# Whole-row loads of the streamed key and value weights, and the order of the loads and stores around the tail multiplications

## The chip, the cores and the metric

The kernel runs on one core of one Trainium2 chip. The metric is the device time of one execution in microseconds (us), from the first to the last instruction. Three runs of the kernel before took 3842.35, 3847.23 and 3854.59 us, so the median is 3847.23 us. The profiled execution took 3842.35 us and its trace spans 3840.6 us.

The engines are named as in the profile: PE is the matrix engine (PEld its weight loads), DVE the vector engine, ACT the scalar engine, POOL GpSimd, and SP the engine that here only issues DMA transfers.

## The reference

Four layers run one after the other on 2048 tokens of width 640: A, B, A, B, each with a layer norm ahead of it and a residual added behind it. All tensors are bf16. The A layer is recurrent over 64 segments of 32 tokens, and each segment takes 8 memory tokens from the one before:

```python
def _A_ref(x, mem0, Wq, Wk, Wv, Wo, seg_len):          # 32 heads of 192
    mem = mem0
    for s in range(n_seg):                             # 64 segments
        h = concatenate([mem, xs], axis=1)             # 8 + 32 tokens
        q, k, v = (einsum('btd,dhe->bhte', h, W) for W in (Wq, Wk, Wv))
        p = softmax(where(mask, q @ k.T * scale, -1e9))
        o = einsum('bhte,hed->btd', p @ v, Wo)
        mem = o[:, :M, :]                              # the chain from segment to segment
        outs.append(o[:, M:, :])
```

The B layer is a linear attention over all 2048 tokens (qkv of width 1920, a small feature map per head, one `kv` sum, then the output product). It can only start on rows whose A output is there.

## The kernel before

**The chain of A.** 6144 output features are worked on in four rounds of 8 heads (`r`, each 1536 columns wide). Most of the weights lie in SBUF for good. For rounds 0 and 3, three of the five contraction pieces of each of Q, K and V share a place (a slot) and so are loaded anew in every segment, as is the output weight of the round that comes last. The last 8 tokens of every segment (the tail) don't take part in the chain's output product. Their attention outputs are stored to DRAM (`otb`) and multiplied with the output weight after the chain.

```python
PW = 1536
def load_slot(m, r, b, whole=False):
    if holds.get((m, b)) != r:
        holds[m, b] = r
        w = PW if whole or m == "Q" else PW // 2
        for h in range(0, PW, w):                       # K and V in the chain: two halves
            nc.sync.dma_start(out=slot[m, b][:, h:h + w], in_=wview[m][:, b, PW * r + h:PW * r + h + w])

def project(hT, ps, m, n, s, steps):                    # round n of segment s
    for i in steps:
        b = (i + KC - ns) % KC if n == 0 else i         # n == 0: the slots first
        w = piece(m, r, b)
        for g in range(4):
            ...                                         # rhs of K and Q: columns of both halves
            nc.tensor.matmul(o[32 * g:32 * g + 32, 0:384], lhsT=hT[:, b, :], rhs=rhs, ...)
        if n == 0 and b >= KC - ns:
            load_slot(m, order[NR - 1], b)              # for the last round of the same segment
```

A segment issues its transfers on SP in this order: Q slots, K slots, V slots (all freed in round 0, read again in round 3), then the six pieces of the last output weight (freed by the first `wo_round`, read by the last):

```python
wo_round(W, order[n - 1], OT, n == 1, False)
if n == 1:
    load_wo(order[L])                                   # six pieces of 320 KB
```

**The start of B.** The stored tails come back in four blocks of 16 segments (1.5 MB each). `fetch` loads a block, `spread` reorders it by four copies, two on ACT and two on DVE, and `multiply` does 48 x 2 matmuls and stores 128 rows to `at_dram` (`attn`). The rows of B are then read back from `attn`, normed (`norm_rows`) and transposed (`turn_rows`).

```python
with tc.issue_after(self.last_load.ins):
    load_rows(0)
fetch, spread, multiply = post
ot = [fetch(tb) for tb in range(2)]
ow = [spread(tb, ot[tb]) for tb in range(2)]
ot += [fetch(tb) for tb in range(2, 4)]
for j in (1, 2, 0):
    nc.sync.dma_start(out=wqkv[:, :, D * j:D * j + D], in_=...)
multiply(0, ow[0], kv_ps[0], side_bank("ps_post"))
ow.append(spread(2, ot[2]))
rows = [norm_rows(b) for b in range(4)]
multiply(1, ow[1], ...)
ow.append(spread(3, ot[3]))
multiply(2, ow[2], ...)
first_xnT = new_xnT()
for b in range(4):
    turn_rows(b, rows[b], first_xnT)
multiply(3, ow[3], ...)
```

Blocks 0 and 2 share one buffer, blocks 1 and 3 the other. The order in which instructions of B stand on an engine is set by the scheduler of the language, so the order of the text is a priority and not a promise. The instructions of one engine then run in that order.

Of the kernel before, what the change touches and what calls it, by code (L numbers as in the profile page):

```python
# [112 lines left out]
class Kernel:  # L113
# [131 lines left out]
    def layer_B(self, x_dram, at_dram, xout_dram, xnext_dram, li, bp, post):  # L245


        nc, tc, KC, D = self.nc, self.tc, self.KC, self.Dm
# [41 lines left out]
        with tc.tile_pool(name=f"B{li}_kv", bufs=1, space=bass.MemoryType.PSUM, reuse_waits="tile") as kvp, \  # L290
# [5 lines left out]
            def side_bank(name):  # L296
                return ptp.tile([P, 512], F32, name=name, tag="side")

            nc.gpsimd.memset(wbd[:], 0.0)
            for i in range(HC):  # L300
                n = len(range(i, H, HC))
                nc.gpsimd.dma_start(out=wbd[DH * i:DH * i + DH, 0:n, DH * i:DH * i + DH],
                                    in_=self.B_w_phi[i:H:HC].rearrange("h d f -> d h f"))
# [45 lines left out]
            def load_rows(g):  # L349
                for b in range(4 * g, 4 * g + 4):  # L350
                    nc.sync.dma_start(out=x2[:, b, :], in_=x_dram[P * b:P * b + P, :])

            def norm_rows(b):
                xt = x2[:, b, :]
                al = als.next()
                nc.sync.dma_start(out=al[:], in_=at_dram[P * b:P * b + P, :])
                nc.gpsimd.tensor_tensor(out=xt, in0=xt, in1=al[:], op=ALU.add)  # L357
                xn = xns.next()
                self.ln_rows(bp, xt, xn, scale=nc.scalar)
                return xn  # L360
# [90 lines left out]

            with tc.issue_after(self.last_load.ins):
                load_rows(0)
            fetch, spread, multiply = post
            ot = [fetch(tb) for tb in range(2)]
            ow = [spread(tb, ot[tb]) for tb in range(2)]
            ot += [fetch(tb) for tb in range(2, 4)]
            for j in (1, 2, 0):
                nc.sync.dma_start(out=wqkv[:, :, D * j:D * j + D],
                                  in_=self.B_wqkv.rearrange("(k p) n -> p k n", p=P)[:, :, D * j:D * j + D])  # L460
            multiply(0, ow[0], kv_ps[0], side_bank("ps_post"))
            ow.append(spread(2, ot[2]))
            rows = [norm_rows(b) for b in range(4)]
            multiply(1, ow[1], kv_ps[1], side_bank("ps_post"))
            ow.append(spread(3, ot[3]))
            multiply(2, ow[2], kv_ps[0], side_bank("ps_post"))
            first_xnT = new_xnT()
            for b in range(4):
# [11 lines left out]
            for sg in range(2):  # L480
                for c in range(NC_):
                    mc, nh = sizes[c], sizes[c] // DH
                    o = kv_out(sg, c).rearrange("p (h f) -> p h f", f=DH + 1)
# [88 lines left out]
    def layer_A(self, xn_dram, at_dram, li, x_raw=None):  # L572
        nc, tc = self.nc, self.tc
        KC, NSEG = self.KC, self.NSEG
        dram = self.dram
        NR = 4
        PW = 1536
        self.kqb_d = dram.tile([NSEG, P, NR, 192], BF16, name=f"kqb{li}")
        self.vb_d = dram.tile([NSEG, NR, 2, 8, 896], BF16, name=f"vb{li}")
        self.otb_d = dram.tile([NSEG, P, 384], BF16, name=f"otb{li}")  # L580
        wview = self.wview
        wov = self.A_Wo.rearrange("h d m -> (h d) m").rearrange("(c p) m -> p c m", p=P)
        low = self.view(0, LATE)
        at = LATE
        res, slot = {}, {}
        for r in (3, 2):
            for m in "KQV":
                for b in range(KC - (SLOTS[m] if r == 3 else 0)):
                    res[m, r, b] = low[:, len(res) * PW:len(res) * PW + PW]
        assert len(res) * PW * 2 == LATE  # L590
        for m, r, b in [(m, 0, b) for m in "KQV" for b in range(KC - SLOTS[m])] + \
                [(m, None, b) for m in "KQV" for b in range(KC - SLOTS[m], KC)] + [(m, 1, b) for m in "KQV" for b in range(KC)]:
            v = self.view(at, 2 * PW)
            at += 2 * PW
            if r is None:
                slot[m, b] = v
            else:
                res[m, r, b] = v
        holds = {}
        wo_mid = self.view(at, 24 * 1280)  # L600
        wo_end = self.view(at + 24 * 1280, 12 * 1280)
        assert at + 36 * 1280 == ARENA
        unread = set(res)

        def load_slot(m, r, b, whole=False):
            if holds.get((m, b)) != r:
                holds[m, b] = r
                w = PW if whole or m == "Q" else PW // 2
                for h in range(0, PW, w):
                    nc.sync.dma_start(out=slot[m, b][:, h:h + w], in_=wview[m][:, b, PW * r + h:PW * r + h + w])  # L610

        def load_matrix(m, r):
            for b in range(KC):
                if (m, r, b) in unread:
                    unread.remove((m, r, b))
                    nc.sync.dma_start(out=res[m, r, b], in_=wview[m][:, b, PW * r:PW * r + PW])
                elif (m, r, b) not in res:
                    load_slot(m, r, b, True)

        early = {(0, 5), (2, 4), (2, 5), (1, 0), (1, 1), (1, 2), (1, 3)}  # L620

        def load_wo(r, into=None, part=range(6)):
            t = into if into is not None else wo_end[:, :] if r in (0, 3) else wo_mid[:, 7680 * (r - 1):7680 * r]
            for k in part:
                tk = t[:, 1280 * k:1280 * k + 1280]
                if r in (0, 3):
                    self.last_load = nc.sync.dma_start(out=tk, in_=self.wo_rows[r // 3, :, 1280 * k:1280 * k + 1280])
                else:
                    nc.sync.dma_start(out=tk.rearrange("p (c m) -> p c m", m=640),
                                      in_=wov[:, 12 * r + 2 * k:12 * r + 2 * k + 2, :])  # L630

        def piece(m, r, b):
            assert (m, r, b) in res or holds[m, b] == r
            return res[m, r, b] if (m, r, b) in res else slot[m, b]

        def lay_out_wo():
            if li == 0:
                self.wo_rows = dram.tile([2, P, 7680], BF16, name="wo_rows")
                for i, r in enumerate((0, 3)):
                    nc.scalar.dma_start(out=self.wo_rows[i].rearrange("p (c m) -> p c m", m=640),  # L640
                                        in_=wov[:, 12 * r:12 * r + 12, :])

        def early_wo():
            for r in (0, 2, 1):
                load_wo(r, part=[k for k in range(6) if (r, k) in early])

        def late_wo(r):
            load_wo(r, part=[k for k in range(6) if (r, k) not in early])

        self.A_pre(xn_dram, li, load_matrix, piece, wo_mid, wo_end, lay_out_wo, early_wo, x_raw)  # L650
        self.A_chain(xn_dram, at_dram, li, load_slot, piece, load_wo, late_wo, wo_mid, wo_end, low)
        self.post_args = at_dram, wo_mid, wo_end, low

# [445 lines left out]
    def post_steps(self, ops):  # L1099

        nc = self.nc
        at_dram, wo_mid, wo_end, low = self.post_args
        wo = [wo_end[:, :], wo_mid[:, 0:7680], wo_mid[:, 7680:15360], low[:, 0:7680]]

        def fetch(tb):
            o = 7680 + 12288 * (tb % 2)
            ot = low[:, o:o + 6144].rearrange("p (s f) -> p s f", f=384)
            nc.sync.dma_start(out=ot, in_=self.otb_d[16 * tb:16 * tb + 16].rearrange("s p f -> p s f"))
            return ot

        def spread(tb, ot):
            o = 7680 + 12288 * (tb % 2)
            ow = low[:, o + 6144:o + 12288].rearrange("p (c q) -> p c q", q=P)
            for k in range(4):
                self.ev.copy(out=ow[:, 12 * k:12 * k + 12, :].rearrange("p c (s t) -> p c s t", t=8),
                             in_=ot[:, :, 96 * k:96 * k + 96].rearrange("p s (c t) -> p c s t", t=8))
            return ow

        def multiply(tb, ow, p0, p1):
            for c in range(48):  # L1120
                lhsT = ow[:, c, :]
                w0 = 640 * (6 * (c % 2) + c % 12 // 2)
                w = wo[c // 12][:, w0:w0 + 640]
                nc.tensor.matmul(p0[:, :], lhsT=lhsT, rhs=w[:, 0:512], start=(c == 0), stop=(c == 47))  # L1124
                nc.tensor.matmul(p1[:, 0:128], lhsT=lhsT, rhs=w[:, 512:640], start=(c == 0), stop=(c == 47))
            ob = ops.tile([P, 640], BF16, name="obB", tag="obB", bufs=2)
            nc.vector.tensor_copy(out=ob[:, 0:512], in_=p0[:, :])
            nc.scalar.activation(out=ob[:, 512:640], in_=p1[:, 0:128], func=ACT.Copy)
            av = at_dram.rearrange("(s t) d -> s t d", t=32)
            nc.gpsimd.dma_start(out=av[16 * tb:16 * tb + 16, 24:32, :], in_=ob[:, :])  # L1130

        return fetch, spread, multiply


# [33 lines left out]
```

## Time and profile before

| | us | share of the span |
|---|---|---|
| span of the trace | 3840.6 | |
| PE busy | 3561.2 | 93% |
| DVE busy | 2327.9 | 61% |
| ACT busy | 2075.0 | 54% |
| POOL busy | 1668.6 | 43% |
| queue 1 (transfers issued on SP), share of 16 DMA engines | | 60.7% |
| first chain of A, from about 212 us to 1629 us | 1417 | 37% |
| second chain of A, from about 2112 us to 3521 us | 1409 | 37% |

The page cuts the span into 40 equal slices and writes the busy share of each as a digit. Groups of instructions follow with their line of the kernel, the names of output and inputs, the shapes, the count, the busy time, the mean of one in ns, and the idle time just ahead of them with what ended it. A wait is written "who line <- what it waited for: us in total, times, longest us". "issue" stands where the profile shows nothing that was waited for. Among the chain's loads the page counts 768 issues of K and 768 of V with 192 KB each; those are the halves.

### The profile page before, as it was taken

To read this page: it belongs to the slowest core of one execution; us is meant where nothing else is said; L and a number is where in the kernel's file an instruction comes from. 1 tells how busy PE (TensorE), PEld (TensorE's weight loads), DVE (VectorE), ACT (ScalarE), POOL (GpSimd) and SP (SyncE) were. 2 spreads that over 40 slices of the span, in tenths; PEclk is the share of its full clock that TensorE was granted. 3 is DMA by queue.
4 is the path that set the end of the run, shared out by engine and by line. 5 is a ranking of instruction groups with operands and counts; after the bars stand their busy time and mean duration, and the time that the engine had idled before them with its cause. 6 is when DMAs were issued, how large, how long until landed. Compare 5 with 4: busy or idle time off the path is not lost. (4 is left out here: it accounts for less than half of the span.)

```text
span 3840.6 us, 167757 instructions
## 1 busy us (share of the span) xinstructions
PE 3561.2 (93%) x70296; PEld 2244.8 (58%) x70312; DVE 2327.9 (61%) x6038; ACT 2075.0 (54%) x5285; POOL 1668.6 (43%) x4375
## 2 busy tenths in 40 slices
PE   7889999999999999989899899999999999999798
PEld 5656566666666565545367556666666666665453
DVE  3546666666666666545643566666666666664464
ACT  2245666556655565536432556566665656664453
POOL 2435454455544454430242444555455454553300
PEclk9999999999999999989899999999999999999898
DMA  9787888888888887840377878888888888889100
GB/s 323 243 266 271 283 281 282 277 268 292 275 281 277 270 288 264 298 134 1 120 246 201 296 268 285 274 285 282 280 283 268 284 272 283 282 278 298 48 1 28
DMA packets 587137, 935.19 MB, mean 243 GB/s; under 512 B 147322, under 2 KB 401802, under 8 KB 586378
## 3 DMA queue, kind: packets, MB, share of 16 engines
q1 hardware_dynamic: 448042, 804.45, 60.7%
q0 software_dynamic: 68672, 90.26, 8.0%
q10 hardware_dynamic: 69664, 29.76, 2.9%
q8 instruction: 551, 9.03, 1.0%
q14 instruction: 208, 1.70, 0.1%
HBM read 855.97 MB, written 72.09 MB: 242 GB/s over the span
## 5 line engine op out<-in xcount | busy, mean ns | idle before, releaser
L884 PE MATMUL ps_qk<-arena,hT 128*32 128x384 bf16 x20480 | 1004.1, 328 | 24.6 <-DMA arena<-in_A_Wk_dram 7.3
L884 PEld LDWEIGHTS <-hT 128*32 128x32 bf16 x30720 | 742.6, 97 | 472.8 <-DVE hT L1094 59.1
L894 ACT ACTIVATE raw<-ps_qk 128x384 bf16<-128x384 f32 x1024 | 503.0, 491 | 442.2 <-PE ps_s L987 248.9
L960 PE MATMUL ps_w<-arena,OT 128*32 128x160 bf16 x24576 | 552.8, 235 | 65.2 <-issue 36.3
L867 POOL DMA_DIRECT2D Vp<-vb x512 | 258.7, 505 | 675.4 <-PE ps_o L934 463.2
L960 PEld LDWEIGHTS <-OT 128*32 128x32 bf16 x24576 | 437.8, 97 | 184.0 <-issue 90.7
L884 PE MATMUL ps_v<-arena,hT 128*32 128x384 bf16 x10240 | 538.4, 330 | 0.6 <-issue 0.5
L899 DVE STREAM_TRANSPOSE KT<-raw 128x384 bf16<-128x384 bf16 x512 | 296.1, 578 | 199.3 <-ACT raw L894 195.3
L902 DVE STREAM_TRANSPOSE QT<-raw 128x256 bf16<-128x256 bf16 x512 | 227.9, 445 | 269.2 <-ACT raw L894 240.6
L855 POOL DMA_DIRECT2D kqb<-kqb x512 | 290.0, 566 | 168.6 <-POOL KT L863 146.6
L915 DVE CAST Vp<-ps_v 64x384 bf16<-64x384 f32 x512 | 286.0, 559 | 99.0 <-ACT Vp L913 84.4
L953 POOL DMA_DIRECT2D otb<-otb x512 | 282.5, 552 | 133.7 <-DVE otb L949 105.0
L913 ACT ACTIVATE Vp<-ps_v 64x384 bf16<-64x384 f32 x512 | 246.3, 481 | 150.9 <-PE ps_v L884 117.5
L940 DVE CAST OT<-ps_o 128x192 bf16<-128x192 f32 x512 | 183.1, 358 | 215.2 <-PE ps_o L934 197.3
L934 PEld LDWEIGHTS <-Vp 80*128 80x128 bf16 x4096 | 182.6, 99 | 189.0 <-issue 128.5
L994 DVE TENSOR_TENSOR E<-E,ps_s 80x320 bf16<-80x320 bf16 x512 | 247.5, 483 | 73.9 <-ACT ps_s L993 69.3
L973 ACT ACTIVATE E<-ps_s 80x320 bf16<-80x320 f32 x512 | 221.8, 433 | 114.6 <-PE ps_s L926 102.0
L934 PE MATMUL ps_o<-E,Vp 80*128 80x80 bf16 x4096 | 235.3, 202 | 26.6 <-issue 4.7
L926 PE MATMUL ps_s<-QT,KT 128*80 128x80 bf16 (+1 forms) x3072 | 234.7, 214 | 22.3 <-DVE KT L899 13.0
L860 POOL COPY QT<-kqb 128x64 bf16<-128x64 bf16 x512 | 125.6, 245 | 283.2 <-PE ps_s L926 279.6
L967 PE MATMUL ps_idle<-arena,ident 128*128 128x384 bf16 x1024 | 235.0, 332 | 5.0 <-issue 5.0
L939 ACT ACTIVATE OT<-ps_o 128x192 bf16<-128x192 f32 x512 | 167.8, 328 | 131.4 <-PE ps_o L934 131.3
(148 smaller groups left out, 5348.5 us busy)
## 6 DMA issues: line engine op xcount, KB each, us to landing
arena<-wo_rows SPq DMA_DIRECT2D x792, 320.0 KB, 5.9
arena<-in_A_Wq_dram SPq DMA_DIRECT2D x430, 384.0 KB, 4.5
arena<-in_A_Wk_dram SPq DMA_DIRECT2D x768, 192.0 KB, 5.4
arena<-in_A_Wv_dram SPq DMA_DIRECT2D x768, 192.0 KB, 5.2
kqb<-arena ACTq DMA_DIRECT2D x16, 1536.0 KB, 11.3
kqb<-kqb POOLq DMA_DIRECT2D x512, 48.0 KB, 5.0
arena<-in_A_Wk_dram SPq DMA_DIRECT2D x46, 384.0 KB, 6.7
arena<-in_A_Wv_dram SPq DMA_DIRECT2D x46, 384.0 KB, 8.2
```

Of the source, the lines that this page charges most:

```text
L855: nc.gpsimd.dma_start(out=kqb[:], in_=self.kqb_d[s, :, r, :])
L867: nc.gpsimd.dma_start(out=Vs[n % 2][64:80, :], in_=self.vb_d[s, r].rearrange("g t f -> (g t) f"))
L884: nc.tensor.matmul(o[32 * g:32 * g + 32, 0:384], lhsT=hT[:, b, :], rhs=rhs, start=(i == 0), stop=(i == KC - 1), tile_position=(0, 32 * g), ...
L894: nc.scalar.activation(out=raw[:], in_=ps[:, 0:384], func=ACT.Copy)
L899: nc.vector.transpose(out=KT[:, :, 0:64], in_=raw[:, :].rearrange("p (c j) -> p c j", j=64))
L913: nc.scalar.activation(out=o, in_=i, func=ACT.Copy)
L915: nc.vector.tensor_copy(out=o, in_=i)
L934: nc.tensor.matmul(O[x][:, 80 * i:80 * i + 80], lhsT=Vs[n % 2][0:80, 448 * x + k:448 * x + k + 128], rhs=E[0:80, 160 * x + 80 * e:160 * x ...
L953: nc.gpsimd.dma_start(out=self.otb_d[s, :, 96 * r:96 * r + 96], in_=otb[:, :, :].rearrange("p c t -> p (c t)"))
L960: nc.tensor.matmul(W[32 * g:32 * g + 32, 0:160], lhsT=OT[:, c, q:q + 32], rhs=w[:, 640 * i + 160 * g:640 * i + 160 * g + 160], start=(firs ...
L967: nc.tensor.matmul(ps[:, 0:384], lhsT=self.ident[:, :], rhs=wo_mid[:, 0:384], start=True, stop=True, skip_group_check=True)
L994: nc.vector.tensor_tensor(out=E[0:80, 0:320], in0=E[0:80, 0:320], in1=rc, op=ALU.mult)
```

## The change

The change has two independent parts.

- The K and V slots of the chain are loaded as whole rows: one transfer of 128 rows of 3072 bytes, where there were two of 128 rows of 1536 bytes. It is meant to give the DMA engines fewer and longer rows and SP fewer issues.
- At the start of B, the tail blocks 2 and 3 are no longer loaded ahead of the three loads of `wqkv`. Loading and spreading of a block are one step again, and the steps of blocks 2 and 3 stand behind the multiplications of blocks 0 and 1. The stores of the multiplied blocks are issued on SP in place of GpSimd. This makes the code simpler, and frees GpSimd of eight issues.

```diff
-            fetch, spread, multiply = post
-            ot = [fetch(tb) for tb in range(2)]
-            ow = [spread(tb, ot[tb]) for tb in range(2)]
-            ot += [fetch(tb) for tb in range(2, 4)]
+            fetch, multiply = post
+            ow = [fetch(tb) for tb in range(2)]
             for j in (1, 2, 0):
                 nc.sync.dma_start(out=wqkv[:, :, D * j:D * j + D], ...)
             multiply(0, ow[0], kv_ps[0], side_bank("ps_post"))
-            ow.append(spread(2, ot[2]))
+            ow.append(fetch(2))
             rows = [norm_rows(b) for b in range(4)]
             multiply(1, ow[1], kv_ps[1], side_bank("ps_post"))
-            ow.append(spread(3, ot[3]))
+            ow.append(fetch(3))
...
-        def load_slot(m, r, b, whole=False):
+        def load_slot(m, r, b):
             if holds.get((m, b)) != r:
                 holds[m, b] = r
-                w = PW if whole or m == "Q" else PW // 2
-                for h in range(0, PW, w):
-                    nc.sync.dma_start(out=slot[m, b][:, h:h + w], in_=wview[m][:, b, PW * r + h:PW * r + h + w])
+                nc.sync.dma_start(out=slot[m, b], in_=wview[m][:, b, PW * r:PW * r + PW])
...
             nc.sync.dma_start(out=ot, in_=self.otb_d[16 * tb:16 * tb + 16].rearrange("s p f -> p s f"))
-            return ot
-
-        def spread(tb, ot):
-            o = 7680 + 12288 * (tb % 2)
             ow = low[:, o + 6144:o + 12288].rearrange("p (c q) -> p c q", q=P)
...
-            nc.gpsimd.dma_start(out=av[16 * tb:16 * tb + 16, 24:32, :], in_=ob[:, :])
+            nc.sync.dma_start(out=av[16 * tb:16 * tb + 16, 24:32, :], in_=ob[:, :])
```

## The prediction

> **What bounds the kernel now.** I read the page first: which engine is full, and where. PE is at nine tenths wherever a chain of A runs. The DMA engines are not far behind there, at eight tenths, and queue 1 (SP's loads) is most of that.
>
> ```profile
> PE   7889999999999999989899899999999999999798
> DMA  9787888888888887840377878888888888889100
> q1 hardware_dynamic: 448042, 804.45, 60.7%
> L884 PE MATMUL ps_qk<-arena,hT 128*32 128x384 bf16 x20480 | 1004.1, 328 | 24.6 <-DMA arena<-in_A_Wk_dram 7.3
> L960 PE MATMUL ps_w<-arena,OT 128*32 128x160 bf16 x24576 | 552.8, 235 | 65.2 <-issue 36.3
> arena<-in_A_Wk_dram SPq DMA_DIRECT2D x768, 192.0 KB, 5.4
> ```
>
> Next, busy times by stretch (columns: stretch and length, busy us and count for PE, PEld, DVE, ACT, POOL, then granted clock, DMA share, GB/s). Well inside the first chain PE works 1280 of 1340 us, and the DMA share is 0.82. So PE bounds the chain, and all that a faster transfer can give back is among the 60 us in which PE stood still.
>
> ```profile
> 260.00:1600.00 1340.00, 1280.01 (x30984) 808.30 (x30976) 883.53 (x2399) 806.64 (x2150) 672.33 (x1847) 1.00 0.82 277
> 1669.00:1679.00 10.00, 0.22 (x2) 0.10 (x1) 4.72 (x16) 2.16 (x9) 6.49 (x11) 0.69 0.23 66
> ```
>
> Then who waits. PE's own waits between 330 and 1600 us are headed by the output product (L960): 20.6 us of "issue" and 9.3 us for its weight `wo_rows`.
>
> ```profile
> PE ps_w L960 <- issue: 20.6, 27, 1.9
> PE ps_w L960 <- DMA arena<-wo_rows: 9.3, 18, 1.8
> ```
>
> Asked over the whole span, line 960 waits 27.1 us for `wo_rows`, in 53 stops:
>
> ```profile
>   DMA arena<-wo_rows: 27.1, 53
> ```
>
> SP's own queue, in contrast, mostly waits for PE to free a slot:
>
> ```profile
> SPq L610 <- PE ps_qk L884: 1161.5, 445, 11.6
> ```
>
> Last, SP's timeline in one segment: after three Q loads come six halves of K, six of V, and the output weight at the end.
>
> ```profile
> 1008.48 1.28 SPq L610 DMA_DIRECT2D arena<-in_A_Wq_dram  x3
> 1009.85 3.65 SPq L610 DMA_DIRECT2D arena<-in_A_Wk_dram  x6
> 1014.52 4.61 SPq L610 DMA_DIRECT2D arena<-in_A_Wv_dram  x6
> 1019.22 3.15 SPq L627 DMA_DIRECT2D arena<-wo_rows  x6
> ```
>
> Taking such landings from the trace for 124 segments, counted from the first Q issue, the medians are: Q landed at 6.0 us, K 10.0, V 13.8, the last output weight 19.5, in a period of 21.5. In the segment above PE reads the K slots in round 3 about 12 us after that point, V about 15, and the last output weight from about 19. The loads have 2 us, 1 us and nothing to spare. The output weight is last in the queue, and it is the one that PE is seen waiting for.
>
> **What the Trainium skill says.** "DMA: Bandwidth & Descriptors", section "Why small descriptors are slow (HBM only)", gives each packet a fixed overhead of about 3 cycles beside 32 bytes a cycle. An estimate from it: two rows of 1536 bytes are 2 x (48 + 3) = 102 cycles, one of 3072 is 99, a gain of 3%. The packet records of this trace say more: median 65 ns for 1536 bytes, 121 ns for 3072, so 130 against 121, 7%. I take the trace's. The same page, "Queues, rings and completion order", says that an engine takes the descriptors of one ring in order and goes round between queues. The landings agree in that Q, K, V and the output weight land in the order of issue. So what shortens K and V brings the output weight forward by as much. Its section "Latency and other measured facts" puts the first byte at some 0.6 us for SP's path and 1 us for GpSimd's. The medians of the issue table are close to that: 2.3 us for the 160 KB `attn` loads on SP and 2.5 us for the 160 KB stores on GpSimd.
>
> **Part one, whole rows.** Each DMA engine moves 8 of a piece's 128 rows and one 4-byte completion (9 ns). Two halves take 2 x (8 x 65 + 9) = 1058 ns, a whole one 8 x 121 + 9 = 977: 81 ns less. By the means, 70.7 ns in the chain for a half row and 131 for a whole one in the first 200 us (the page's densest loading of such rows), it is 92 ns. Six pieces a segment give 0.5 to 0.6 us. In all, 768 pieces x 90 ns is 69 us of every engine, 1.8% of the span, so queue 1 should go from 60.7% to about 58.9%. Its packets fall by 768 x 128 = 98304 and 768 x 16 = 12288 completions, from 448042 to about 338,500 with the eight stores added.
>
> Of this nothing counts while PE has its data anyway. It counts where PE waits for `wo_rows`. I went through those waits above 0.25 us, segment by segment, and gave each segment back its wait, at most 0.6 us: 6.2 us in the first chain and 6.0 in the second, as most segments that wait lose 0.3 to 0.7 us, and a few lose 1 to 2. The first segments of the chains also wait for K slots, some 3.3 and 4.0 us on PE; I give those 0.6 each. Sum: about **-13 us**. The 768 issues saved on SP, 0.33 to 0.41 us each, are worth nothing of themselves: SP waits for PE or for room in the ring, and a full ring means that the DMA engines are busy.
>
> **Part two, the start of B.** Three things here stop PE, each in both layers, the third barely.
>
> (a) In the chain's last segment the first copies of `spread(0)` stand on DVE and ACT ahead of the chain's own work and wait for block 0; the transpose of K stands behind them, and PE is idle for 6.56 us. The lines of the wait:
>
> ```profile
> 1620.38 0.56 DVE L84 COPY arena<-arena 128x1536 bf16<-128x1536 bf16 x1 [6.44 <-issue]
> 1621.57 0.73 PE L926 MATMUL ps_s<-QT,KT 128*80 128x80 bf16 x6 [6.56 <-DVE KT L899]
> ```
>
> The change keeps `fetch(0)` and its copies first, so I expect the stall to stay, shorter by the 0.6 us that K and V give: -1 us for two layers.
>
> (b) From 1669 to 1679 PE has 0.22 us of work (the second stretch above). It waits for ACT to copy transposes out, and ACT's queue has norms of the next rows ahead of that. Those wait for `attn` rows that wait for the store of block 1. In the second layer the chain of waits shows it:
>
> ```profile
> 3558.19 0.63 issue
> 3558.82 2.41 DMA attn<-obB
> ...
> 3562.36 2.23 DMA arena<-attn
> 3564.91 2.08 POOL arena L357 x2
> ...
> 3570.78 0.60 ACT arena L86
> 3571.42 0.69 PE ps_x L163 x5
> ```
>
> The store on SP needs no place in GpSimd's queue (0.63 us) and lands some 0.3 us sooner: -1 us a layer. Against it, stores of block 0 now share SP's ring with the blocks 2 and 3 and `wqkv` and land behind them; in the first layer that store took 5.9 us even on its own queue. I put +2 us a layer there. Net: +2 us for both.
>
> (c) Blocks 2 and 3 come behind 2.4 MB of `wqkv`, some 7.5 us. Block 2 landed at 1642.7; it would land near 1650. The copies take 3 us, and its multiplication starts near 1655, as multiplications of 13 us run on end from 1629. Hidden, with 2 us to spare. `wqkv` itself is read at 1694. If block 2's load stands behind the rows of `attn` on SP, it lands at 1655 and costs 3 us. I add +1 us.
>
> **Sum**: -13 - 1 + 2 + 1 = -11 us, from 3847 to about **3837 us**.
>
> **The rivals.**
> 1. *Longer rows delay others.* Small loads and stores (`kqb`, `Vp`, `otb`) and PE's instruction fetches (queue 8, 16 KB each) take turns with these rows. In the trace a `Vp` load lands in 4.8 to 5.0 us among rows of 1536 bytes and in 5.2 to 5.4 among rows of 2560. The "issue" stops of L960, 36.3 us, come at no piece boundary and look like late instructions; with half as much again they cost 15 us, which would undo the gain. For it: halves were chosen for K and V. Against it: Q and the output weight are long rows already. It makes 3845 to 3855.
> 2. *The gain is hidden.* PE reaches the output product earlier, waits there less, and then waits for something else, as the hand-over to the next segment (`hT`, L1094). Then the time stays within 3 us. Against it: the wait for `wo_rows` lies ahead of that hand-over, on the same path.
> 3. *The scheduler places B anew.* The 6.5 us stop may go, double (a second block's copies in the chain), or the 10 us stop may change by half. That is up to 13 us either way on two layers, and can't be read from this trace.
>
> **Range and chances.** Part one is -13, give or take 10 by rival 1; part two 2, give or take 10 by rival 3; single runs differ by 12 us. Together 8 in 10 lie within 25 us: 3812 to 3862. 2% is 77 us, more than all PE waits in both chains' interiors that I could name, so "within 2%" has 0.95, faster 0.03, slower 0.02.
>
> **What would show it.** Right: queue 1 near 59%, `wo_rows` waits of L960 down from 27 to about 14 us, "issue" near 36, the DMA copies' stop at 6 us and the transposes' stop at 10. Wrong: rows of 3072 bytes that take over 140 ns on average in the chain, "issue" stops above 50 us, or a stop at the end of the chain or among the multiplications that is new or gone.

## The result and the profile after

The changed kernel takes 3892.57 us (median of 4 runs, 3888.04 to 3899.86); the kernel before took 3850.87 us beside it. The ratio is 1.0113, with a 95% interval of 1.0087 to 1.014. So the change costs 1.1%, some 43 us, and I had predicted 3837 us, at most 3862.

The page of the changed kernel, in the same lines as before (lines of the kernel have moved: L956 is the output product, L880 the projections):

```profile
PE   7889999999999999889899899999999999998898
...
DMA  9787877777777777840377877777778777788200
...
q1 hardware_dynamic: 338602, 805.71, 57.7%
...
L956 PE MATMUL ps_w<-arena,OT 128*32 128x160 bf16 x24576 | 552.9, 236 | 88.3 <-issue 79.8
...
arena<-in_A_Wv_dram SPq DMA_DIRECT2D x430, 384.0 KB, 8.4
```

The DMA engines have less to do, as intended: queue 1 went from 60.7% of a span of 3840.6 us to 57.7% of 3887.3, which is 89 us less for each engine. PE's busy time is the same (3565 us against 3561). But the idle time ahead of the output product grew, and "issue" makes up nearly all of it: 79.8 us where it was 36.3. Busy time by stretch shows the place, the inside of the first chain, with 22 us less PE work in the same 1340 us:

```profile
260.00:1600.00 1340.00, 1258.23 (x30416) 799.17 (x30408) 866.51 (x2353) 789.49 (x2112) 659.68 (x1811) 0.99 0.77 273
```

PE's waits between 330 and 1600 us, and below them line 956 over the whole span:

```profile
PE ps_w L956 <- issue: 38.5, 39, 2.1
PE ps_qk L880 <- DVE hT L1090: 6.8, 43, 0.2
PE ps_o L930 <- issue: 5.6, 5, 1.4
PE ps_qk L880 <- issue: 3.7, 9, 0.9
```

```profile
  DMA arena<-wo_rows: 7.5, 8
```

The wait for the output weight fell from 27.1 us to 7.5, further than I had expected. "Issue" stops took its place and more, and they now turn up at the projections and at the attention too.

By stage, from PE's first and last work in each (us):

| | first chain | start of B | B | A's preparation | second chain | start of B | last B |
|---|---|---|---|---|---|---|---|
| before | 1416.6 | 65.0 | 253.9 | 164.9 | 1408.7 | 65.8 | 253.2 |
| after | 1440.2 | 62.2 | 253.8 | 166.0 | 1442.6 | 62.4 | 247.1 |

The two chains lost 57.5 us. The other stages gained 11.

**What "issue" is here.** I took the stops above 0.25 us in which PE runs neither a matmul nor a weight load and which the profile puts down to "issue", in both chains, and compared them with the transfers of queue 8, which moves 551 blocks of 16 KB. In the kernel before, 57 of 59 such stops end 1.15 to 1.85 us after such a block has been moved; in the changed one, 129 of 130. By chance it would be about one in eight, as a block is moved every 5.6 us. These stops are called fetch stops below. Counted through PE's stream, the numbers of the instructions that they hold up differ by multiples of 256 within a chain, for all but two of the 129. The trace has 141,012 instructions of PE, weight loads included, which is 550.8 blocks of 256. So PE stands still because its next 256 instructions have not come. The Trainium skill, "Runtime: NRT & Kernel Launch", section "Instruction fetch mechanics", describes just this refill, 256 instructions in 16 KiB through a DMA queue of the sequencer's own, and calls its cost mostly hidden. The size agrees with this trace; "mostly hidden" doesn't hold here: these stops take 46 us of the chains before, and 124 us after.

The output product suffers most, and it uses up instructions fastest: 48 matmuls and as many weight loads in 1.0 us, while a projection runs 20 of each in that time. Its weight is also under way just then; the runs below don't part the two.

**How late a fetch is.** As a gauge I use the time from one fixed instruction in each block of 256, the same in all runs, to the start of the block transfer that follows. Its zero is arbitrary; its differences count. Over both chains it is 3.12 us on average before and 3.58 after. Two executions with the same halves, the kernel before and the start of B alone, differ by 0.13. The transfer itself is as long as it was (1.07 us each), so the wait ahead of it is what grew.

### The profile page after: what moved, and what is told of

The parts are those of the page before. It is cut to its first block, busy times and chain, and to the rows that moved or that the text cites. A ratio compares the mean times of both kernels' runs of the same rounds, so it can differ in the third digit from the quotient of the medians.

```text
span 3887.3 us, 166590 instructions
## 1 busy us (share of the span) xinstructions
PE 3565.1 (92%) x70296; PEld 2257.0 (58%) x70312; DVE 2329.2 (60%) x6038; ACT 2066.2 (53%) x5285; POOL 1665.0 (43%) x4367
## 3 DMA queue, kind: packets, MB, share of 16 engines
q1 hardware_dynamic: 338602, 805.71, 57.7%
## 5 line engine op out<-in xcount | busy, mean ns | idle before, releaser
L880 PE MATMUL ps_qk<-arena,hT 128*32 128x384 bf16 x20480 | 1010.0, 328 | 38.1 <-DVE hT L1090 16.1
L880 PEld LDWEIGHTS <-hT 128*32 128x32 bf16 x30720 | 748.6, 97 | 501.3 <-DVE hT L1090 65.1
L956 PE MATMUL ps_w<-arena,OT 128*32 128x160 bf16 x24576 | 552.9, 236 | 88.3 <-issue 79.8
L956 PEld LDWEIGHTS <-OT 128*32 128x32 bf16 x24576 | 440.4, 98 | 206.2 <-issue 109.8
L880 PE MATMUL ps_v<-arena,hT 128*32 128x384 bf16 x10240 | 544.3, 330 | 9.3 <-issue 8.7
L844 ACT ACTIVATE Vp<-ps_w 32x160 bf16<-32x160 f32 x512 | 150.7, 294 | 207.0 <-DVE wt L1089 200.2
```

What stands on the lines that cost most here:

```text
L956: nc.tensor.matmul(W[32 * g:32 * g + 32, 0:160], lhsT=OT[:, c, q:q + 32], rhs=w[:, 640 * i + 160 * g:640 * i + 160 * g + 160], start=(firs ...
```

## The experiments

Theory: longer transfers hold up the instruction fetches. The main rival was the new order at the start of B. Further down the question becomes what about the transfers it is: the rows (A), the bytes of a transfer (B, D), or the bytes that SP has in flight (C). This table gives all runs. "Fetch stops" and "wo waits" (for the output weight) count stops above 0.25 us in both chains of the one profiled execution, "gauge" is the average of the gauge in them; the ratio is to the kernel before, run beside each.

| run | us | ratio (95%) | fetch stops, us (count) | wo waits, us | gauge, us |
|---|---|---|---|---|---|
| kernel before | | | 46.0 (57) | 25.0 | 3.12 |
| the change | 3892.57 | 1.0113 (1.0087 to 1.014) | 124.1 (129) | 7.5 | 3.58 |
| whole rows alone | 3897.47 | 1.0107 (1.0064 to 1.015) | 121.6 (129) | 7.2 | 3.66 |
| start of B alone | 3842.54 | 0.9959 (0.9941 to 0.9977) | 51.9 (62) | 21.8 | 3.25 |
| short rows, big transfers | 3910.31 | 1.0142 (1.0105 to 1.0179) | 144.5 (167) | 7.8 | 3.75 |
| long rows, small transfers | 4263.32 | 1.1045 (1.1003 to 1.1088) | 180.9 (141) | 103.8 | 4.18 |
| quarters | 4586.41 | 1.1895 (1.1849 to 1.1941) | 0 | 398.9 | 2.45 |
| output weight in halves | 3871.96 | 1.0049 (1.0033 to 1.0066) | 1.7 (4) | 46.0 | 2.73 |
| whole, four in flight | 3889.51 | 1.0089 (1.0055 to 1.0124) | 73.1 (82) | 34.0 | 3.31 |
| whole, three in flight | 4041.26 | 1.0492 (1.046 to 1.0525) | 54.4 (51) | 133.5 | 2.92 |
| halves, four in flight | 4273.06 | 1.109 (1.1057 to 1.1123) | 16.5 (15) | 281.5 | 2.70 |
| V whole, K in halves | 3842.69 | 0.9988 (0.9969 to 1.0006) | 97.5 (97) | 9.2 | 3.40 |
| whole, output weight in halves | 3816.58 | 0.9909 (0.9888 to 0.9929) | 41.7 (59) | 15.9 | 3.25 |
| no K and V reloads | 3762.06 | 0.976 (0.9735 to 0.9785) | 27.0 (29) | 7.5 | |

**Which part costs: one part at a time.** The kernel before with whole rows:

```diff
-                w = PW if whole or m == "Q" else PW // 2
+                w = PW
```

> Part one alone: the kernel before, with K and V slots loaded as whole rows; the start of B as before. Theory (whole rows make PE's instruction fetches late in the chains): both chains lose as in the changed kernel, +57 us in sum by the stages of its trace, so about 3905 us, with the long 'issue' stops of PE near 124 as there, and wo_rows waits near 8 us. Rival (the new order at the start of B is what costs): about 3838 us, as I had predicted for part one, with the stops as before.

The changed kernel with the halves put back (`whole` is true in the stages outside the chains, here and below, and the lines that hand it over are left out):

```diff
-                nc.sync.dma_start(out=slot[m, b], in_=wview[m][:, b, PW * r:PW * r + PW])
+                w = PW if whole or m == "Q" else PW // 2
+                for h in range(0, PW, w):
+                    nc.sync.dma_start(out=slot[m, b][:, h:h + w], in_=wview[m][:, b, PW * r + h:PW * r + h + w])
```

> Part two alone: the changed kernel with K and V slots in halves again. Theory: the chains take what they took before (1417 and 1409 us) and the stages behind them what they took in the changed kernel (some 3 us less in each start of B, 6 us less in the last B layer), so about 3838 us. Rival (part two costs): 3880 us or more.

Whole rows alone cost 1.07%, all of the loss: the chains took 2886 us against 2825, the fetch stops rose by 76 us and the waits for the output weight fell by 18, which leaves 58 of the 61 us. PE's line over the whole span, 36.3 us in the kernel before:

```profile
PE ps_w L960 <- issue: 73.8, 82, 2.3
```

The start of B alone gains 0.41%, 16 us. Its waits on PE over the whole span:

```profile
PE ps_w L958 <- issue: 37.3, 51, 1.9
PE ps_w L958 <- DMA arena<-wo_rows: 23.5, 44, 1.4
```

These are close to the numbers of the kernel before (36.3 and 27.1). The rival is out. The two parts alone add up to a loss of 0.66%, where both together lose 1.13%; the intervals are wide enough for that to be noise.

**Rows or transfers.** Next, the two things that doubled together were pulled apart. First, rows of 1536 bytes as before, but the halves of all three slots of a matrix in one transfer (576 KB):

```diff
+                if whole or m == "Q":
+                    nc.sync.dma_start(out=slot[m, b], in_=wview[m][:, b, PW * r:PW * r + PW])
+                elif b == KC - 1:
+                    n, w = SLOTS[m], PW // 2
+                    o = slots_at[m]
+                    all3 = self.view(o, 2 * PW * n).rearrange("p (b f) -> p b f", b=n)
+                    for h in range(0, PW, w):
+                        nc.sync.dma_start(out=all3[:, :, h:h + w], in_=wview[m][:, KC - n:KC, PW * r + h:PW * r + h + w])
```

> Changed kernel, but each of K and V loads its three slots by two transfers of 576 KB, each with 1536-byte rows: short rows, a third of the issues of the halves. Theory A (the length of a row sets how long a fetch waits): fast as part two alone, 3838 us give or take 8, stops as before (about 59). Theory B (the bytes of one transfer, or the bytes that SP has queued, set it): slow as the changed kernel or slower, 3893 us or more.

It is as slow as the change or slower (the intervals overlap), with more fetch stops, although its rows are as short as before:

```profile
PE ps_w L965 <- issue: 87.8, 96, 2.4
...
PE ps_qk L889 <- issue: 15.4, 28, 1.1
...
PE ps_w L965 <- DMA arena<-wo_rows: 7.9, 10, 1.6
```

So the length of a row, which my prediction had looked at, is not what costs here (theory A falls). Second, long rows in small transfers:

```diff
+                n = P if whole or m == "Q" else P // 2
+                for p in range(0, P, n):
+                    nc.sync.dma_start(out=slot[m, b][p:p + n, :], in_=wview[m][p:p + n, b, PW * r:PW * r + PW])
```

> Changed kernel, but each piece of K and V by two transfers of 64 partitions with 3072-byte rows, 192 KB each: long rows, small issues. Theory A (row length): slow as the changed kernel, about 3893 us, with about 124 long stops. Theory B (bytes per transfer): fast as part two alone, about 3838 us.

Both theories missed, and this run can't choose between them: its transfers into 64 of the 128 partitions moved more slowly. The records of 3072-byte rows in the chain average 183 ns, against 135 in the changed kernel; without the rows of Q, which are loaded as before, they take some 199 against 128 (parted by their order). The weights starve (waits of 104 us for the output weight), and the fetch stops are the longest of all, with transfers of 192 KB.

**Size of a transfer, or bytes in flight.** The compiled program gives SP's transfers eight semaphores in turn, and each waits for the one eight before it. So SP has at most eight transfers out, whatever their size: 8 halves are 1.5 MB, 8 whole pieces 3 MB. Doubling the transfer doubled what can queue ahead of a fetch. What did queue there rose less: with K or V under way, 1 us after the gauge's start, SP had 1.7 MB out on average before and 2.35 after, and over all fetches of the chains 9% met more than 2 MB before and 41% after. The following runs change the bytes in flight.

K and V in quarters (96 KB each), by `PW // 4`:

> Part two with K and V pieces in quarters: four transfers of 96 KB, rows of 768 bytes. After the halves-in-big-transfers run was slow, the bytes of a transfer are what counts. If so, an instruction fetch waits less still than among halves (2.9 us against 3.1 on the scale of the fetch delays among K and V rows), and PE's long 'issue' stops fall below 50. Against it more time per byte (rows of 768 bytes took 36 to 41 ns, four of them 150 to 160 against 141): the output weight lands 0.5 us later and its waits double to 40 us. In sum 3835 to 3860 us. If the transfer size is not it: stops as with halves.

The output weight in halves, beside K and V in halves:

```diff
-                    self.last_load = nc.sync.dma_start(out=tk, in_=self.wo_rows[r // 3, :, 1280 * k:1280 * k + 1280])
+                    for h in (0, 640):
+                        self.last_load = nc.sync.dma_start(out=tk[:, h:h + 640],
+                                                           in_=self.wo_rows[r // 3, :, 1280 * k + h:1280 * k + h + 640])
```

> Part two alone, and the six pieces of the last output weight as twelve transfers of 160 KB. If smaller transfers let instruction fetches through, the stops at the output product (36 us, 46 times) fall by a third or more, while its weight lands some 0.4 us later, so that the waits for it go from 22 to about 32 us: 3835 to 3845 us. If not, only the second happens: 3850 us.

Both did away with the fetch stops, far more thoroughly than I had said, and both lost time, the quarters very much. With quarters:

```profile
PE ps_w L958 <- DMA arena<-wo_rows: 401.2, 513, 3.4
PE ps_v L882 <- DMA arena<-in_A_Wv_dram: 77.0, 118, 2.3
```

With the output weight in halves:

```profile
PE ps_w L960 <- DMA arena<-wo_rows: 69.6, 194, 2.1
```

Eight transfers of 96 KB are 768 KB. The last piece of V landed 18.2 us after the first Q issue on average, against 13.9 before, and the stretch from 260 to 1600 us moved 219 GB/s in place of 277. My expectation had counted the longer time per byte (0.5 us a segment) and not that so few bytes are out while SP waits for a landing. The output weight in halves is the mild form: fetch stops 1.7 us, waits for the weight 46, and 69.6 with those under 0.25 us. Its chains took 2855 us against 2828 with the start of B alone: beside the waits, PE's busy time in them is 34 us longer, most of it at the output product, which the stops of the table don't show.

Whole pieces, but a slot load waits for the fourth last slot load (for the third last in the second run, with 3 in place of 4):

```diff
-                nc.sync.dma_start(out=slot[m, b], in_=wview[m][:, b, PW * r:PW * r + PW])
+                d = nc.sync.dma_start(out=slot[m, b], in_=wview[m][:, b, PW * r:PW * r + PW])
+                if flow and len(flow) >= 4:
+                    tc.add_manual_dep(d.ins, flow[-4].ins.name,
+                                      mybir.DependencyInfo(mybir.DependencyClass.Sync, mybir.DependencyReason.DATA),
+                                      reason="flow")
+                flow.append(d)
```

> Changed kernel with whole rows, but a slot load waits until the fourth last slot load has landed, so at most 4 x 384 KB are in flight, the bytes of 8 halves; the program itself allows 8 transfers, as it has eight semaphores for SP's transfers. Theory C (a fetch waits behind all bytes in flight): as with halves, about 3842 us and some 60 long stops. Theory D (a fetch waits for a turn, and a turn is one transfer's share on an engine, 0.98 us whole and 0.53 us half): slow as the changed kernel, about 3893 us, some 120 stops.

> As the run with whole rows and four slot loads in flight, but with three (1152 KB). Theory C: the fetch delay among K and V rows falls from 3.3 us at four (4.1 in the changed kernel) to below 3.0, and 'issue' stops of both chains from 85 us to 60 or less; the weights starve more instead, waits for the output weight above 60 us, so 3900 us or more in sum. Theory D (a turn of one transfer): delay and stops back at the changed kernel's 4.1 us and 127 us.

And halves, four in flight, by the same lines:

> Part two alone with halves, but at most four of the halves in flight (768 KB). Theory C: fewer stops than 60, some 30, and up to 20 us less than part two alone (3842), if K and V are not late through it. Theory D: stops as before, the time as with part two alone or up to 15 us more, as the engines run dry at times.

By the clock, the run with four whole pieces looks like theory D (3889.51 us), and the stops did not fall all the way to 60. By its stops it is theory C: with the same transfer of 384 KB, fetch stops went from 124 to 73 us, then to 54 with three in flight. The gauge among the K and V rows went from 4.14 us to 3.33 and 2.63; halves before had 3.08. What is left of the stops sits mostly at the output product, whose weight's transfers were not held back. With three in flight all "issue" stops are 75 us, where I had put 60 or less. The time did not follow: with four in flight, the fetch stops fell by 51 us and the waits for the output weight took 27 of that back, and the rest went in pieces that I did not take apart (7 us for `Vp`, 6 us more PE busy, gaps under 0.15 us). For four in flight:

```profile
PE ps_w L961 <- issue: 52.5, 66, 2.0
PE ps_w L961 <- DMA arena<-wo_rows: 35.2, 68, 2.1
```

With halves, four in flight, the fetch stops are 16.5 us and the waits for the output weight take 281 us of PE's time. "Up to 15 us more" was wrong by far, for the same reason as with the quarters.

The gauge against the bytes that SP had in flight, at 1 us after the gauge's start, in four of seven bins (us; the transfer of K and V in brackets):

| in flight | before (192 KB) | change (384 KB) | short rows (576 KB) | four in flight (384 KB) |
|---|---|---|---|---|
| nothing | 2.2 | 1.7 | 1.8 | 2.2 |
| 0.5 to 1 MB | 2.7 | 3.2 | 3.2 | 3.2 |
| 1.5 to 2 MB | 3.5 | 3.8 | 3.9 | 3.4 |
| 2 to 2.5 MB | 4.0 | 4.6 | 4.7 | 4.3 |

Within a row the runs differ by 0.5 to 0.7 us; down a column the gauge rises by 1.8 to 2.9. The rise is not even: below 0.5 MB, a bin of 20 to 32 fetches a run, the gauge is about 3.0 to 3.5. Of the rise of the average from the kernel before to the change, some seven tenths (0.34 us, by the averages of all bins) come from more fetches that meet more bytes; the rest, 0.13 us at equal bytes, is no more than two runs with halves differ by. So most of the effect is the bytes in flight. Their number alone does not set the wait: in the run with long rows in small transfers, whose rows moved more slowly, the gauge with 1.5 to 2 MB out is about 1 us longer than before. Whether the size of one transfer adds something is open. So is the way in which the engines choose between the queues.

**Between the two: V whole, K in halves.**

> Part two with K in halves and V whole. Theory C: between part two alone and the changed kernel, 'issue' stops of both chains about 95 us against 64 and 127, some 3865 us. A rival in which only one of the matrices matters: near 3842 or near 3890.

The fetch stops, 97.5 us, lie between as expected, and so do the chains, 2858 us against 2828 and 2883. The time, 3842.69 us at the median, is better than the 3865 that I had put there, with a ratio that can't be told from the kernel before. The profiled execution, from which the stops are, took 3860 us and is one of the slowest of the twelve, which lie between 3839 and 3864; why they spread so is open.

**Whole K and V, output weight in halves.** Most stops sit where PE uses up instructions fastest, at the end of a segment, while the output weight is under way. So the big transfers belong early and the small ones late; the edit is the changed kernel with the diff of the output weight above.

> Changed kernel (K and V whole) with the six pieces of the last output weight as twelve transfers of 160 KB. Theory C (an instruction fetch waits longer the more bytes SP has in flight): the stops fall at the output product's end, from 127 us of 'issue' in both chains to about 70; the weight lands some 0.8 us later than in the changed kernel, so waits for it go from 8 to about 25 us. In sum some 40 us less than the changed kernel, about 3850 us. Rival (the stops come from the K and V rows alone): 'issue' stays above 110 us and the time near 3900.

```profile
PE ps_w L958 <- DMA arena<-wo_rows: 20.7, 50, 1.3
PE ps_w L958 <- issue: 20.6, 32, 2.3
...
PE ps_qk L882 <- issue: 9.1, 22, 1.0
```

3816.58 us, faster than the kernel before by 0.9% and than any other version here that computes all: fetch stops of 42 us with waits for the weight of 16. I had expected 3850. Whole K and V rows give back most of the lead that the halves of the output weight cost: its last piece lands 19.9 us after the first Q issue on average, against 19.6 before and 20.5 with halves everywhere. Of the profiled execution's 28 us, the chains make 12 (2813 us against 2825), as the stops and waits say. Another 11 are in the last B layer, where PE's granted clock was 0.97 against 0.92 in the kernel before, and can't be credited to the transfers.

**Without the K and V reloads.**

```diff
-                nc.sync.dma_start(out=slot[m, b], in_=wview[m][:, b, PW * r:PW * r + PW])
+                if whole or m == "Q":
+                    nc.sync.dma_start(out=slot[m, b], in_=wview[m][:, b, PW * r:PW * r + PW])
```

> Changed kernel without the K and V slot loads of the chains: both rounds that share a slot use the weights that the stage before the chain left there, so its output is another. All else is as in the changed kernel. It measures what those loads cost at all. Theory C: with less in flight the 'issue' stops fall from 127 us in both chains to below 35 (13 of them at the chains' ends are no fetches), no wait for the output weight is left, and the time is about 3785 us. If the stops have a cause other than loads in flight, 'issue' stays near 127 us and the time near 3880.

This kernel leaves out those loads and so multiplies with the weights of the wrong round. Its fetch stops are 27 us, a fifth of the change's. PE's own waits over the span:

```profile
PE ps_w L957 <- issue: 11.4, 15, 1.9
...
PE ps_w L957 <- DMA arena<-wo_rows: 7.7, 10, 1.6
```

My "below 35 us" was for all "issue" stops, which are 43 us, and a wait for the output weight is left, where I had expected none. The time is 23 us below what I had expected.

## Why the prediction was wrong, step by step

- **The step that failed is the sum of part one**, which has no term for late instructions. I had them in the first rival, "with half as much again they cost 15 us"; they went from 46 to 124 us in the chains, 78 us more. The reason lies behind the step on SP's issues, "a full ring means that the DMA engines are busy", which stopped short. SP's limit here is eight transfers, not bytes, so twice the transfer let twice the bytes stand ahead of an instruction fetch, and with K or V under way there were 2.35 MB in place of 1.7. And rival 1 looked at rows; the run with short rows in big transfers shows it is not the rows.
- The transfer arithmetic was right in its direction and a little low. Queue 1 lost 89 us of every engine where I had 69 (3.0 points for 1.8, as the span grew too), its packets fell to 338,602 (338,500), rows of 3072 bytes average 135 ns in the chain (below the 140 I had set), and the last output weight lands 18.8 us after the first Q issue at the median, where it was 19.5. The waits for `wo_rows` went to 7.5 us, not 14. So the gain of part one is there, 17.5 us in the chains, and is lost under 78.
- Part two was right in its places and wrong in sign. I had +2 us from the copies' stop, the store and the block order; alone it gains 16 us (9 to 23 by its interval). The term that failed is the +2 us a layer for the stores of block 0, which I had put behind the blocks 2 and 3 and `wqkv` in SP's ring. SP issued the store of block 0 ahead of block 2: it landed 16.4 us after the first chain's end, where it was 21.7, and block 1's at 35.1 where it was 40.0. The lines of the store of block 1, before and after; the first chain ended at 1629.0 and 1653.0 us:

```profile
1666.70 0.54 POOL L1130 DMA_DIRECT2D attn<-obB  x1 [1.97 <-ACT ln_sd L232]
```

```profile
1685.70 0.54 SPq L1122 DMA_DIRECT2D attn<-obB  x1
```

  The path of the store itself matters little: 2.4 us to landing at the median, where it was 2.5; I had put it 0.3 us sooner. My 2.3 and 2.5 us were landings of 160 KB and no first bytes, so they do not confirm the figures for first bytes that they stand beside. The copies still stand ahead of the chain's work, in two stops of together 4.9 us where I had 6:

```profile
1642.59 0.41 PE L917 MATMUL ps_s<-mask_st,ident 80*80 80x320 bf16 x1 [2.21 <-issue]
1645.70 0.73 PE L922 MATMUL ps_s<-QT,KT 128*80 128x80 bf16 x6 [2.70 <-DVE KT L895]
```

  The stop at the transposes went from 10.0 us to 7.4, in place of some 11; PE's wait from 1653 to 1716 us:

```profile
PE ps_x L163 <- ACT arena L86: 7.4, 1, 7.4
```

  The blocks behind `wqkv` are hidden, as I had it: PE multiplies without a stop over blocks 0 to 2. The two starts of B make 6 of the gain. Six to eight us more come out of the last B layer (253.2 us before, 247.1 after, 244.8 with part two alone), whose code is the same. About 2 of them are less idle time, which nearly all runs with part two share and which may be the scheduler's other order (rival 3). The rest is PE's busy time, 217.0, 213.7 and 210.8 us for the same 1198 matmuls, at granted clocks of 0.92, 0.93 and 0.94 in that stage. In other runs with part two the stage took 250.7 us at 0.91 and 241.9 us at 0.97. That part is not shown to come from the change.
- Rival 2 (the gain is hidden) is small: the waits for `hT` at the projections, those under 0.15 us included, went from 12 to 18 us in the chains. Rival 3 is bound up with part two's gain of 16 us; no run parts them. The range fell short by 31 us because I gave rival 1 a spread of 10.

## What to carry to other kernels

A stop of "issue" on an engine with a dense instruction stream is a reading to take seriously: compare where such stops end with the instruction queue's transfers before calling bigger transfers free. What can queue ahead of an instruction fetch is the number of transfers in flight times their size, and a kernel sets both; too much made the instructions late here, and too little (768 KB) starved the loads, which cost more. It is worth trying the big transfers where the engine uses few instructions a microsecond and the small ones where it uses many; here that gained 12 us in two chains.

## What the runs showed of the hardware that I had not expected

- An instruction block's transfer took 1.04 to 1.15 us on average, whatever the run, and at the fetch stops PE went on 1.15 to 1.85 us after it had ended. With nothing of SP's in flight the fetch began 1.8 to 2.9 us earlier than with 2 to 2.5 MB in flight.
- In transfers into 64 partitions each, the 3072-byte rows of K and V took some 199 ns, in transfers into 128 some 128; the kernel took 4263 us against 3893.
- With at most eight quarters of K and V in flight (768 KB), the chain moved 219 GB/s, with eight halves (1.5 MB) 277. The granted clock over that stretch was lower too, 0.90 with quarters against 1.00 before; that PE's idle time brought it down is not shown.
